# Forming P-Q in SBUF by an accumulating transfer instead of two matmuls, in 62 pair steps of a Fourier mix with a squared-ReLU feed-forward

## The chip, the cores and the metric

The kernel runs on one core of a Trainium2 chip. TensorE (PE in the profile; its weight loads are PEld) multiplies, VectorE (DVE) and ScalarE (ACT) work element by element, GpSimd (POOL) and SyncE (SP) issue the transfers. The metric is the device time of one execution in microseconds (us): 633.91, the median of three runs (633.72 to 635.05).

## The reference

```python
def _attn_ref(x):                      # x: (8, 3008, 256) float32
    X = np.fft.fft(x, axis=1)
    X = np.fft.fft(X, axis=2)
    return X.real.astype(np.float32)

def _moe_ref(x, w_in, w_out):          # x: (24064, 256), w_in: (256, 2048), w_out: (2048, 256)
    h = np.maximum(x @ w_in, 0.0)
    return (h * h @ w_out).astype(np.float32)
```

The real part of a two-dimensional Fourier transform of each of 8 batches goes, row by row, through a feed-forward layer with squared ReLU.

## The kernel before

**What is multiplied.** The transform over the 256 features is folded into the first weight matrix: the tile `gh` holds, for each of the 2048 hidden units, a cosine part (index 0), a sine part (index 1) and the sine part times -2 (index 2), over 128 rows d. The transform over the sequence gives `Z`, kept as two tiles of 128 rows d: `zc` (cosine) and `zs` (sine). Row 0 of `zs` has no sine term and carries instead the cosine term of d = 128. With P = `gh[0]`ᵀ`zc` and Q = `gh[1]`ᵀ`zs`, the hidden values of sequence row k are P + Q. Those of the mirrored row S - k are P - Q, except that the term of d = 128 keeps its sign. So one column of Z serves two rows of the output. The factor in `gh[2]` is -2 for every d but 0, and 0 there (`turn2`), so that adding `gh[2]`ᵀ`zs` to P + Q gives just that.

**Windows and steps.** The 12040 columns are cut into 25 windows, w = 0 to 24; windows 6 to 23 are 512 columns wide. A window has 8 pair steps, s = 0 to 7; each forms two chunks of 128 hidden units for all columns of the window, in one PSUM tile `ph` of 128 x 1024 float32 (two such tiles take turns). In a step of the kernel before:

- `pq(s)`: four matmuls of 512 columns (L684, L685) give P + Q;
- `square(s, 0)`: ScalarE takes the ReLU out of PSUM into `h1` (L694; three buffers), VectorE squares it into the first half of `h2` (L696);
- `others(s)`: what is spread over the steps. Always the second layer of the *previous* window: `ffn2_steps` (L596), 16 matmuls of 256 columns a step, two jobs of 8, the first over hidden chunks 0 to 7 and the second over 8 to 15, so that the first group of a window reads all of the previous window's `h2` in step 0. At odd steps ScalarE moves the result to `osb` (L611), and SyncE stores it. Further the Z matmuls of the next window (L478, in `z_steps`, with copies on ScalarE and VectorE), and the folding of a batch, below;
- `turn(s)`: two matmuls of 512 columns with `gh[2]` (L690) turn `ph` into P - Q; they must wait until ScalarE has read P + Q;
- `square(s, 1)`: the same as above, read backwards, into the second half of `h2`.

Both tiles of `h2` and of `ph` alternate. The program is written in its final order: within each engine instructions run in the order in which they are recorded.

**Folding a batch.** In windows 5, 8, 10, 13, 16 and 19 (`fold_at`) VectorE also folds a whole batch (`fold_steps`): L349, L358, L353, L361, L368, L375, L379, one or so a step. In step 2, right behind L353, GpSimd issues the load of the next batch (`load_x`, L125 and L130: one direct transfer and two gathers, 1.5 MB of float16 in SBUF; for two of the batches one of these is patched at its edge, L147 or L141, after a wait for the gather). Window 19 has no next batch. In step 6 GpSimd writes `ev` to a scratch tensor (L381), and in step 7 it waits for that and reads it back by four transfers (L389, L391). In windows 6, 9, 12, 15, 18 and 21 (`late_at`) VectorE folds what came back (L404, L415).

All transfers that GpSimd issues go to one software queue (q0 in the profile); the stores of SyncE go to another.

Of the kernel before, what the change touches and what calls it, by code (L numbers as in the profile page):

```python
# [28 lines left out]
def kernel(  # L29
# [14 lines left out]
    nc = tc.nc  # L44
    B, S, D = x.shape
    _, F = moe_w_in.shape
# [7 lines left out]
    NFC = F // P  # L54
    WN = 512

    FIRST = [240, 512, 376, 376, 512, 448]
    R23 = float(2.0 ** 23)

    RQ = (1, 3, 5, 0, 2, 4)  # L60

# [11 lines left out]
    wins = []  # L73
    g = 0
    while g < TOT:
        n = min(FIRST[len(wins)] if len(wins) < len(FIRST) else WN, TOT - g)
        wins.append((g, n))
        g += n
    NW = len(wins)

    def win_of(col):
        return max(w for w in range(NW) if wins[w][0] <= col) if col < TOT else NW
# [17 lines left out]
    const = ctx.enter_context(tc.tile_pool(name="const", bufs=1))  # L100
    tmp = ctx.enter_context(tc.tile_pool(name="tmp", bufs=2))
# [8 lines left out]
    ps_h = ctx.enter_context(tc.tile_pool(name="ps_h", bufs=2, space=bass.MemoryType.PSUM))  # L110
    ps_o = ctx.enter_context(tc.tile_pool(name="ps_o", bufs=2, space=bass.MemoryType.PSUM))
# [56 lines left out]
    perm = [const.tile([P, P], F16, name=f"perm{i}") for i in range(2)]  # L168
# [3 lines left out]
    nc.gpsimd.memset(idx["c"][0:2, :], P - 3)  # L172
    idx["f"] = iota([P, 1], [[1, 1]], -1, 1, "idx_f")
    nc.gpsimd.memset(idx["f"][0:1, :], 0)
    w16 = [const.tile([P, 2, F // 2], F16, name=f"w16_{i}") for i in range(2)]
    for i in range(2):
        nc.gpsimd.dma_start(out=w16[i], in_=moe_w_in[:, i * F // 2 : (i + 1) * F // 2].rearrange("(c p) f -> p c f", p=P))
    wout16 = const.tile([P, NFC, D], F16, name="wout16")
# [2 lines left out]
    def small(shape, name):  # L181
        return const.tile(shape, F32, name=name)
# [22 lines left out]
    def table_steps(e):  # L205
# [31 lines left out]

# [44 lines left out]
    at = const.tile([P, 2, P + 1], F32, name="at")  # L282
    for c in range(2):
        nc.scalar.activation(at[:, c, :], drow, AF.Copy, bias=R23, scale=dvs[:, c : c + 1])
    nc.vector.tensor_scalar(out=at, in0=at, scalar1=-R23, scalar2=-float(D), op0=ALU.add, op1=ALU.mult)
    for c in range(2):
# [141 lines left out]
    gh = const.tile([P, 3, F], F16, name="gh")  # L428
# [17 lines left out]
    def gh_turn(cc):  # L446
        f0 = cc * 512
        nc.vector.tensor_scalar(out=gh[:, 2, f0 : f0 + 512], in0=gh[:, 1, f0 : f0 + 512], scalar1=turn2[:, 0:1], scalar2=None, op0=ALU.mult)
# [3 lines left out]
    def zwin(w):  # L452
        if w not in zc:
            zc[w] = zp.tile([P, WN], F16, name="zc", tag="zc")
            zs[w] = zp.tile([P, WN], F16, name="zs", tag="zs")
        return zc[w], zs[w]
# [101 lines left out]
    for cc in range(1, F // 512):  # L558
        gh_turn(cc)

    def store(osb, p0, g0, m, minus, eng=nc.sync):

        for b, k0, kstep, n, c0 in runs:
            il, ih = max(g0, c0) - c0, min(g0 + m, c0 + n) - 1 - c0
            if minus and k0 in (0, H):
                il = max(il, 1)
            cnt = ih - il + 1
            if cnt <= 0:
                continue
            if minus:  # L570
                lo = p0 + (m - 1) - (c0 + ih - g0)
                row = b * S + S - (k0 + kstep * ih)
            else:
# [56 lines left out]
    def fold_jobs(i):  # L630
        f = folds[i] = fold_steps(i)
        return [f["d_even"], f["n_cos"], f["d_odd"], f["n_sin"], f["odds"], f["nyq"], f["even"], f["back"]]

    fold_at, late_at = {}, {}
    for i in range(2, B):
        fold_at[win_of(col_of[i, 0]) - 2] = i
        late_at[win_of(col_of[i, 1]) - 2] = i
    NST = NFC // 2
    old = None
    for w in range(NW):  # L640
        g0, wn = wins[w]
        h2 = h2p.tile([P, NFC, 2 * WN], F16, name="h2", tag="h2")
        zcw, zsw = zwin(w)

        lo, hi = 0, NST - 1
        at = [[] for _ in range(NST)]
        post = [[] for _ in range(NST)]
        if w == 0:
            at[2] = [f0s["even"], f0s["back"]]
        elif w == 1:  # L650
            fj = fold_jobs(1)
            at = [[f] for f in fj[0:5]] + [[], [], []]
            post[5] = fj[5:6]
            lo, hi = 6, 7
        elif w == 2:
            te = table_steps(1)
            at = [[folds[1]["even"], lambda: te["freq"](), lambda: te["args"](0)], [lambda: te["turns"](0)], [lambda: te["mods"](0)],
                  [lambda: te["absm"](0)], [lambda: te["sins"](0)], [lambda: te["coss"](0)], [], [lambda: te["weigh"]()]]
            for st in range(4):
                at[st + 3] = at[st + 3] + f0s["late"][st : st + 1]  # L660
            at[7].append(folds[1]["back"])
        elif w in fold_at:
            fj = fold_jobs(fold_at[w])
            at = [[f] for f in fj[0:5]] + [[], fj[6:7], fj[7:8]]
            post[5] = fj[5:6]
        elif w == win_of(col_of[1, 1]) - 1:
            for st in range(4):
                at[st] = folds[1]["late"][st : st + 1]
            lo = 4
        if w in late_at:  # L670
            for st in range(4):
                at[st + 2] = at[st + 2] + folds[late_at[w]]["late"][st : st + 1]
        zj, zl = [], []
        for u in need[w + 1]:
            zu = z_steps(u)
            zj += [(zu, 0, 0), (zu, 1, 0), (zu, 0, 1), (zu, 1, 1)]
        f2 = ffn2_steps(*old) if old else []
        phs = {}

        def pq(s):  # L680
            ph = phs[s] = ps_h.tile([P, 2, 512], F32, name="ph", tag="psh")
            for a in range(2):
                f0 = (2 * s + a) * P
                nc.tensor.matmul(ph[:, a, 0:wn], gh[:, 0, f0 : f0 + P], zcw[:, 0:wn], start=True, stop=False)  # L684
                nc.tensor.matmul(ph[:, a, 0:wn], gh[:, 1, f0 : f0 + P], zsw[:, 0:wn], start=False, stop=True)  # L685

        def turn(s):
            for a in range(2):
                f0 = (2 * s + a) * P
                nc.tensor.matmul(phs[s][:, a, 0:wn], gh[:, 2, f0 : f0 + P], zsw[:, 0:wn], start=False, stop=True, skip_group_check=True)  # L690

        def square(s, sg):
            h1 = h1p.tile([P, 2, 512], F16, name="h1", tag="h1")
            nc.scalar.activation(h1[:, :, 0:wn], phs[s][:, :, 0:wn], AF.Relu)  # L694
            hv = rev_dim(h1[:, :, 0:wn], 2) if sg else h1[:, :, 0:wn]
            nc.vector.tensor_tensor(h2[:, 2 * s : 2 * s + 2, sg * wn : (sg + 1) * wn], hv, hv, op=ALU.mult)  # L696

        def others(s):
            for j in at[s]:
                j()  # L700
            for j in spread(f2, s, NST):
                j()
            for j in post[s]:
                j()
            if s == lo:
                zl[:] = [j for zu, part, h in zj for j in zu(part, h)]
            if s >= lo:
                for j in spread(zl, s - lo, hi - lo) if s < hi else []:
                    j()


        ng = 2 if w == 0 or wins[w - 1][1] < 384 < wn else 1
        for s0 in range(0, NST, ng):
            ss = range(s0, s0 + ng)
            for s in ss:
                pq(s)
            for s in ss:
                square(s, 0)
            others(s0)
            for s in ss:  # L720
                turn(s)
            for s in ss:
                square(s, 1)
            for s in ss[1:]:
                others(s)
        old = (w, h2)
    for j in ffn2_steps(*old, tail=True):
        j()
# [30 lines left out]
```

## Time and profile before

| | |
|---|---|
| median of three runs | 633.91 us |
| span of the profiled execution | 632.0 us |
| TensorE busy | 615.9 us, 97% |
| ScalarE busy | 457.4 us, 72% |
| VectorE busy | 369.5 us, 58% |
| GpSimd busy | 76.5 us, 12% |
| window 0 starts at | 21.7 us |
| window 6 starts at | 140.1 us |
| window 24 starts at | 595.5 us |

A window starts with its first L684 matmul. The profile gives for each group of instructions its line, engine, output and inputs, count, busy time and mean duration, and the idle time of the engine just ahead of it with what ended that idle time. A matmul of 512 columns shows a duration of 379 ns, but the next one starts some 215 ns after it: they overlap, so the distance of starts is what one costs in a dense stream. The same holds to a smaller degree on ScalarE and VectorE, where independent neighbours overlap by about 0.1 us.

### The profile page before, as it was taken

The page shows a single profiled execution, that of the slowest core. Times are in us where ns is not written, and L with a number is a line of the kernel's source. Part 1 is how long each engine was busy: PE and PEld are TensorE (multiplying, and loading weights), DVE is VectorE, ACT ScalarE, POOL GpSimd, SP SyncE. Part 2 cuts the span into 40 slices and gives each one's busy share as a digit, 9 for nine tenths or more (in the row PEclk, how much of TensorE's full clock was granted, in tenths as well). Part 3 has the DMA queues.
Part 4 walks back from the last instruction along what each step waited for, and adds up shares of the span by engine and source line. Part 5 has one row for each costly group of instructions (what it writes and reads, how often), then busy time and mean ns, then how long its engine had stood idle before and what let it go on. Part 6 is the DMA issues. An engine that isn't in the chain of part 4 may idle for free.

```text
span 632.0 us, 11586 instructions
## 1 busy us (share of the span) xinstructions
PE 615.9 (97%) x4548; PEld 439.1 (69%) x4548; DVE 369.5 (58%) x604; ACT 457.4 (72%) x610; POOL 76.5 (12%) x125
## 2 busy tenths in 40 slices
PE   5899999999999999999999999999999999999997
PEld 2457776776777767767777677777677776777786
DVE  7887656765457557645576455854557555454430
ACT  7787778777777677767777777777777777777662
POOL 5352200022002200220011100030000200000000
PEclk9999999999999999999999999999999999999999
DMA  8936211172112711631127211262111311111112
GB/s 146 211 82 127 85 34 34 50 164 78 36 43 58 184 46 42 144 97 35 51 44 160 74 52 39 59 151 73 40 31 55 111 34 47 38 46 35 49 54 65
DMA packets 36525, 47.52 MB, mean 75 GB/s; under 512 B 4216, under 2 KB 30328, under 8 KB 36472
## 3 DMA queue, kind: packets, MB, share of 16 engines
q0 software_dynamic: 9344, 22.14, 17.6%
q1 hardware_dynamic: 26899, 24.44, 12.7%
q8 instruction: 35, 0.57, 0.4%
q10 hardware_dynamic: 228, 0.21, 0.1%
q14 instruction: 19, 0.15, 0.1%
HBM read 33.63 MB, written 27.84 MB: 97 GB/s over the span
## 4 chain that ended last, share of the span: by engine, by line
PE 93%; DVE 3%; ACT 2%; issue 1%; POOL 0%; ACTq 0%; POOLq 0%; DVEq 0%
PE po L596 51%; PE ph L684 12%; PE ph L685 12%; PE ph L690 12%; PE pz L478 4%; ACT h L694 1%; PE pw L301 1%; DVE h L696 1%; PE pg L436 0%; ACT cos L259 0%; DVE fe L349 0%; DVE fo L353 0%; ACT sin L248 0%; ACT gh L440 0%; DVE od L368 0%
## 5 line engine op out<-in xcount | busy, mean ns | idle before, releaser
L694 ACT ACTIVATE h<-ph 128x1024 f16<-128x1024 f32 (+4 forms) x400 | 368.4, 974 | 80.0 <-PE ph L690 72.1
L696 DVE TENSOR_TENSOR h<-h 128x1024 f16<-128x1024 f16 (+4 forms) x400 | 262.4, 660 | 231.6 <-ACT h L694 228.2
L596 PE MATMUL po<-wout,h 128*128 128x256 f16 (+1 forms) x3024 | 361.6, 273 | 0.0
L596 PEld LDWEIGHTS <-h 128*128 128x128 f16 (+1 forms) x3024 | 296.8, 98 | 71.3
L684 PE MATMUL ph<-zc,gh 128*128 128x512 f16 (+4 forms) x400 | 145.9, 366 | 1.1 <-ACT h L694 0.8
L685 PE MATMUL ph<-zs,gh 128*128 128x512 f16 (+4 forms) x400 | 145.9, 366 | 0.4 <-ACT zs L487 0.4
L690 PE MATMUL ph<-zs,gh 128*128 128x512 f16 (+4 forms) x400 | 112.8, 366 | 2.0 <-ACT h L694 1.5
L611 ACT ACTIVATE osb<-po 128x512 f32<-128x512 f32 (+3 forms) x95 | 54.9, 582 | 57.4 <-PE po L596 52.4
L685 PEld LDWEIGHTS <-gh 128*128 128x128 f16 x400 | 39.1, 98 | 43.8 <-issue 2.5
L684 PEld LDWEIGHTS <-gh 128*128 128x128 f16 x400 | 39.0, 98 | 41.8 <-issue 0.5
L690 PEld LDWEIGHTS <-gh 128*128 128x128 f16 x400 | 37.2, 97 | 12.7 <-issue 4.3
L421 POOL COPY xt<-xt 128x2 f16<-128x2 f16 x16 | 2.5, 186 | 173.2 <-DVE xt L404 173.2
L130 POOL DMA_INDIRECT xo<-in_x_dram,idx_r x15 | 22.1, 1471 | 4.6 <-issue 4.6
L125 POOL DMA_DIRECT2D xo<-in_x_dram x8 | 6.0, 751 | 109.8 <-DVE fo L353 109.8
L483 ACT ACTIVATE es<-pz 128x376 f32<-128x376 f32 (+1 forms) x32 | 15.4, 481 | 5.3 <-PE pz L478 5.2
L391 POOL DMA_INDIRECT rb<-scr,idx_r x16 | 18.5, 1158 | 4.9 <-issue 4.9
L487 ACT ACTIVATE zs<-pz 128x376 f16<-128x376 f32 (+23 forms) x27 | 8.5, 358 | 9.9 <-PE pz L478 9.9
L349 DVE TENSOR_TENSOR fe<-xo 128x3072 f16<-128x3072 f16 x8 | 14.3, 1786 | 1.6 <-DMA xo<-in_x_dram,idx_r 1.3
L353 DVE TENSOR_TENSOR fo<-xo 128x3072 f16<-128x3072 f16 x8 | 14.2, 1779 | 0.0
L494 DVE SCALAR_TENSOR_TENSOR zc<-es,pz 128x376 f16<-128x376 f32 (+20 forms) x26 | 9.4, 392 | 7.2 <-ACT zc L487 7.0
L301 PE MATMUL pw<-spn 128*128 128x384 f16 x30 | 8.2, 448 | 5.2 <-DVE spn L290 5.2
L389 POOL DMA_DIRECT2D rb<-scr x16 | 8.8, 551 | 33.4 <-DMA scr<-ev 33.0
(106 smaller groups left out, 220.4 us busy)
## 6 DMA issues: line engine op xcount, KB each, us to landing
out_dram<-osb SPq DMA_DIRECT2D x77, 128.0 KB
xo<-in_x_dram POOLq DMA_DIRECT2D x7, 768.0 KB, 7.0
scr<-ev POOLq DMA_DIRECT2D x8, 390.0 KB, 4.4
rb<-scr POOLq DMA_DIRECT2D x16, 130.0 KB, 5.1
out_dram<-osb SPq DMA_DIRECT2D x12, 94.0 KB
w<-in_moe_w_in_dram POOLq DMA_DIRECT2D x2, 512.0 KB, 10.0
wout<-in_moe_w_out_dram POOLq DMA_DIRECT2D x1, 1024.0 KB, 14.5
out_dram<-osb SPq DMA_DIRECT2D x8, 75.0 KB
```

What stands on the lines that cost most here:

```text
L130: nc.gpsimd.indirect_dma_start(out=flat(q), out_offset=None, in_=bass.AP(tensor=x.tensor, offset=0, ap=[[XW, B * S * D // XW], [1, XW]]), ...
L301: nc.tensor.matmul(pw[:, 0 : 3 * P], spn[:, 0, 0, :], spn.rearrange("p c r d -> p (c r d)")[:, 0 : 3 * P], start=True, stop=True)
L391: nc.gpsimd.indirect_dma_start(out=rb[:, q].rearrange("p r d -> p (r d)"), out_offset=None, in_=bass.AP(tensor=src.tensor, offset=src.offs ...
L478: nc.tensor.matmul(ps[:, o0:o1], lhs, tab, start=(h == 0 and k == 0), stop=last, skip_group_check=True)
L483: nc.scalar.activation(es[:, 0:n], ps[:, 0:n], AF.Copy, bias=0.0, scale=1.0)
L596: nc.tensor.matmul(po[0:m, j * D : (j + 1) * D], h2[:, fc, q : q + m], wout16[:, fc, :], start=(fc == 0), stop=(fc == NFC - 1))
L611: nc.scalar.activation(osb[0:mm].rearrange("p s d -> p (s d)")[:, lo:hi], po[0:mm, lo:hi], AF.Copy, bias=0.0, scale=HS * HS)
L684: nc.tensor.matmul(ph[:, a, 0:wn], gh[:, 0, f0 : f0 + P], zcw[:, 0:wn], start=True, stop=False)
L685: nc.tensor.matmul(ph[:, a, 0:wn], gh[:, 1, f0 : f0 + P], zsw[:, 0:wn], start=False, stop=True)
L690: nc.tensor.matmul(phs[s][:, a, 0:wn], gh[:, 2, f0 : f0 + P], zsw[:, 0:wn], start=False, stop=True, skip_group_check=True)
L694: nc.scalar.activation(h1[:, :, 0:wn], phs[s][:, :, 0:wn], AF.Relu)
L696: nc.vector.tensor_tensor(h2[:, 2 * s : 2 * s + 2, sg * wn : (sg + 1) * wn], hv, hv, op=ALU.mult)
```

## The change

In 62 pair steps (windows 6 to 23: steps 0, 2, 3 and 5 of a window without a batch fold, steps 1 and 3 of windows 8, 10, 13, 16 and 19) the two `turn` matmuls are gone. Such a step now runs thus:

- `half_q`: two matmuls give Q alone in `ph`. ScalarE copies -2Q to `sn[:, 0]`. VectorE forms the missing d = 128 term in `sn[:, 1]` by two `tensor_scalar` (row 0 of `zs`, spread over 128 partitions in `eb`, times `wv`, twice row 0 of `gh[1]` per hidden unit). GpSimd issues a transfer that adds `sn[:, 1]` onto `sn[:, 0]` (128 x 1024 float16, SBUF to SBUF). `sn` has two buffers, which take the place of the loaded first weight matrix.
- `others` as before, then `half_p`: two matmuls add P; ScalarE copies P + Q to the first half of `hd`.
- two steps later, `half_d`: VectorE adds `hd` and `sn[:, 0]` into the second half of `hd` backwards, takes the maximum with 0 over both halves (128 x 2048), and squares both into `h2`.

In steps that keep the old form, the first square of steps 1 and 4 (or of 0, 4 and 6 in the five windows with a fold) moves from VectorE to ScalarE. Window 3 gets 16 one-column matmuls for `wv`. In step 7 of each window from 5 to 22 SyncE issues the transfer that fills `eb`.

```diff
+    MANY, FEW = (0, 2, 3, 5), (1, 3)
+    SQ_MANY, SQ_FEW = (1, 4), (0, 4, 6)
...
+    def row_weights():
+
+        pv = ps_o.tile([P, 512], F32, name="pv", tag="po")
+        for fc in range(NFC):
+            nc.tensor.matmul(pv[:, fc : fc + 1], gh[:, 1, fc * P : (fc + 1) * P], perm[0][:, P - 1 : P], start=True, stop=True)
+        nc.vector.tensor_scalar(out=wv, in0=pv[:, 0:NFC], scalar1=2.0, scalar2=None, op0=ALU.mult)
...
+    def row_spread(w):
+
+        wn = wins[w][1]
+        t = eb[w] = tmp.tile([P, WN], F16, name="eb", tag="kf")
+        src = zwin(w)[1][0:1, 0:wn]
+        nc.sync.dma_start(out=t[:, 0:wn], in_=bass.AP(tensor=src.tensor, offset=src.offset, ap=[list(src.ap[0]), [0, P], [1, wn]]))
...
+    def halved(w):
+
+        if wins[w][1] < WN or w < 6:
+            return ()
+        return FEW if w in fold_at else MANY
...
-            nc.vector.tensor_tensor(h2[:, 2 * s : 2 * s + 2, sg * wn : (sg + 1) * wn], hv, hv, op=ALU.mult)
+            if sg == 0 and s in by_act:
+                nc.scalar.activation(h2[:, 2 * s : 2 * s + 2, 0:wn], hv, AF.Square)
+            else:
+                nc.vector.tensor_tensor(h2[:, 2 * s : 2 * s + 2, sg * wn : (sg + 1) * wn], hv, hv, op=ALU.mult)
+
+        two = halved(w)
+        by_act = () if not two else SQ_FEW if w in fold_at else SQ_MANY
+        sns, hds = {}, {}
+
+        def half_q(s):
+            ph = phs[s] = ps_h.tile([P, 2, 512], F32, name="ph", tag="psh")
+            for a in range(2):
+                f0 = (2 * s + a) * P
+                nc.tensor.matmul(ph[:, a, 0:wn], gh[:, 1, f0 : f0 + P], zsw[:, 0:wn], start=True, stop=True)
+            i = ROT[0] % 2
+            sn = sns[s] = const.tile([P, 2, 2, WN], F16, name=f"sn{i}", tag=f"w16_{i}")
+            nc.scalar.activation(sn[:, 0, :, 0:wn], ph[:, :, 0:wn], AF.Copy, bias=0.0, scale=-2.0)
+            for a in range(2):
+                nc.vector.tensor_scalar(out=sn[:, 1, a, 0:wn], in0=eb[w][:, 0:wn], scalar1=wv[:, 2 * s + a : 2 * s + a + 1], scalar2=None, op0=ALU.mult)
+            nc.gpsimd.dma_start(out=sn[:, 0, :, 0:wn].rearrange("p a n -> p (a n)"), in_=sn[:, 1, :, 0:wn].rearrange("p a n -> p (a n)"), accum_op=ALU.add)
+
+        def half_p(s):
+            ph, sn = phs[s], sns[s]
+            for a in range(2):
+                f0 = (2 * s + a) * P
+                nc.tensor.matmul(ph[:, a, 0:wn], gh[:, 0, f0 : f0 + P], zcw[:, 0:wn], start=False, stop=True, skip_group_check=True)
+            hd = tmp.tile([P, 2, 2 * WN], F16, name="hd", tag=("tt", "tm")[ROT[0] % 2])
+            ROT[0] += 1
+            nc.scalar.activation(hd[:, :, 0:wn], ph[:, :, 0:wn], AF.Copy, bias=0.0, scale=1.0)
+            hds[s] = hd
+
+        def half_d(s):
+            sn, hd = sns[s], hds.pop(s)
+            nc.vector.tensor_tensor(rev_dim(hd[:, :, wn : 2 * wn], 2), hd[:, :, 0:wn], sn[:, 0, :, 0:wn], op=ALU.add)
+            nc.vector.tensor_scalar(out=hd, in0=hd, scalar1=0.0, scalar2=None, op0=ALU.max)
+            nc.vector.tensor_tensor(h2[:, 2 * s : 2 * s + 2, :], hd, hd, op=ALU.mult)
...
+            if s0 == hi and w + 1 < NW and halved(w + 1):
+                row_spread(w + 1)
+            if s0 in two:
+                half_q(s0)
+                if s0 - 2 in hds:
+                    half_d(s0 - 2)
+                others(s0)
+                half_p(s0)
+                continue
             for s in ss:
                 pq(s)
             for s in ss:
                 square(s, 0)
+            if s0 - 2 in hds:
+                half_d(s0 - 2)
             others(s0)
...
+        for s in sorted(hds):
+            half_d(s)
```

More of the change, by code (lines that the diff above doesn't have):

```diff
@@ L174 @@
     nc.gpsimd.memset(idx["f"][0:1, :], 0)
-    w16 = [const.tile([P, 2, F // 2], F16, name=f"w16_{i}") for i in range(2)]
+    w16 = [const.tile([P, 2, F // 2], F16, name=f"w16_{i}", tag=f"w16_{i}") for i in range(2)]
     for i in range(2):
@@ L559 @@
         gh_turn(cc)
+    wv = small([P, NFC], "wv")
+    def row_weights():
[3 more added lines that the diff above has]
+        nc.vector.tensor_scalar(out=wv, in0=pv[:, 0:NFC], scalar1=2.0, scalar2=None, op0=ALU.mult)
+    eb = {}
+    def row_spread(w):
[3 more added lines that the diff above has]
+        nc.sync.dma_start(out=t[:, 0:wn], in_=bass.AP(tensor=src.tensor, offset=src.offset, ap=[list(src.ap[0]), [0, P], [1, wn]]))
     def store(osb, p0, g0, m, minus, eng=nc.sync):
@@ L638 @@
     NST = NFC // 2
+    def halved(w):
+        if wins[w][1] < WN or w < 6:
+            return ()
+        return FEW if w in fold_at else MANY
+    ROT = [0]
     old = None
@@ L672 @@
                 at[st + 2] = at[st + 2] + folds[late_at[w]]["late"][st : st + 1]
+        if w == 3:
+            at[0].append(row_weights)
         zj, zl = [], []
```

## The prediction

> **What bounds the kernel now.** I read the engine totals and the chain of waits first.
>
> ```profile
> span 632.0 us, 11586 instructions
> PE 615.9 (97%) x4548; PEld 439.1 (69%) x4548; DVE 369.5 (58%) x604; ACT 457.4 (72%) x610; POOL 76.5 (12%) x125
> PE 93%; DVE 3%; ACT 2%; issue 1%; POOL 0%; ACTq 0%; POOLq 0%; DVEq 0%
> ```
>
> TensorE sets the end. Next the windows one by one (busy us of PE, PEld, DVE, ACT, POOL, each with its count; clock; DMA share; GB/s): windows 8 (fold and load), 12 (no Z matmuls) and 16 (fold, load, Z).
>
> ```profile
> 190.51:214.90 24.39, 24.39 (x180) 17.27 (x179) 18.19 (x25) 17.48 (x21) 3.98 (x4) 1.00 0.55 124
> 292.94:317.27 24.33, 24.33 (x177) 17.21 (x176) 12.98 (x20) 17.46 (x21) 0.63 (x4) 1.00 0.14 44
> 393.41:418.96 25.55, 25.55 (x199) 18.41 (x198) 19.05 (x27) 19.20 (x27) 5.16 (x6) 1.00 0.43 85
> ```
>
> TensorE has no gap in any of them, and its clock is full. So a matmul less is worth its whole pitch, and any new wait of TensorE is paid in full. The timeline of two neighbouring steps gives the pitch:
>
> ```profile
> 269.90 0.38 PE L684 MATMUL ph<-zc,gh 128*128 128x512 f16 x1
> 270.10 1.94 ACT L694 ACTIVATE h<-ph 128x1024 f16<-128x1024 f32 x2 [1.20 <-PE ph L690]
> 270.11 0.38 PE L685 MATMUL ph<-zs,gh 128*128 128x512 f16 x1
> 270.76 1.91 PE L596 MATMUL po<-wout,h 128*128 128x256 f16 x16
> ```
>
> A 512-column matmul costs 0.215 us (starts at 269.90, 270.11), the 16 of L596 1.75. An old step is 6 x 0.215 + 1.75 = 3.04 us, a new one 4 x 0.215 + 1.75 = 2.61. ScalarE's two reads (of `turn` of the step before, and of this step) end 2.14 us after the step's start (270.10 + 1.94 = 272.04).
>
> **Gain.** 62 x 2 x 0.215 = 26.7 us of TensorE. The 16 matmuls for `wv` cost about one weight load each (L596's PEld, 98 ns): +1.6.
>
> **What hides the new work.** VectorE, per new step: two multiplies of 512 (the L448 row below; two of them took 0.64), an add like L696 (0.69), a maximum of 2048, a square of 2048. The square: L696 takes 0.692 for 1024 and L349 1.786 for 3072, so 0.69 + 0.53 = 1.22. No row has the maximum; between 0.63 (slope from L265's 0.315 for 377 to L448's 0.34 for 512) and four L448 (1.36), I take 0.70, since both rows are of its kind. That is 3.25 for the two squares of 0.69 it replaces: +1.9 a step. Window 12: 13.0 + 4 x 1.9 - 2 x 0.7 = 19.2 of 22.6 us; window 16: 19.05 + 3.8 - 2.1 = 20.8 of 24.7. It fits. ScalarE keeps its count of large reads and gains 2 or 3 squares of about 1.0 (like L694, 1.03 for this shape): window 12 19.5 of 22.6, window 16 22.2 of 24.7. It fits too, so neither becomes the bound by its sum. What decides is when things are ready.
>
> **Small waits of ScalarE (+6).** Before, `turn` came 0.865 + 1.75 = 2.61 after the step's start, ScalarE was ready at 2.14. Now `half_p` comes at 0.43 + 1.75 = 2.18: slack 0.04. Behind an odd step (its `osb` copy, 0.60) ScalarE starts some 0.1 later, and in step 2 it carries a square of step 1 besides (about 0.4). Some 0.45 a window, in 13 windows: 6.
>
> **End of the 13 windows with four new steps (+10).** `half_d(5)` stands behind `square(7, 0)` on VectorE. Step 7 starts at 4 x 2.61 + 3 x 3.04 = 19.57; ScalarE is through at 21.7, VectorE's square at 22.4, then 0.69 + 0.70 + 1.22 with its own waits: 25.05. The next window starts at 22.6, and its second job of L596 reads chunk 10 (step 5's) at 22.6 + 0.43 + 0.87 + 0.22 = 24.1. TensorE waits 0.95 in 7 such windows; 0.55 in 5 before an old first step; 0.8 before window 24: 10.2.
>
> **The transfer.** No row shows an accumulating transfer. From issue to landing a plain one on this queue (`scr`, 390 KB; ours writes 256 and reads it twice):
>
> ```profile
> L448 DVE TENSOR_SCALAR gh<-gh,turn x4: 337/341/376, 20.9 to 24.1; 128x512 f16<-128x512 f16 x4
> DMA to landing us min/median/max: 2.4/4.3/7.5
> ```
>
> I take the median, 4.3, as it is the size nearest, and keep 2.4 and 7.5. Issued at 2.2 it lands 6.5 after its step's start; `half_d(0)` can't start before 8.0 (VectorE squares step 1 first), so the wait costs nothing there, with 1.4 to spare. But the queue is shared:
>
> ```profile
> 201.51 0.75 POOL L125 DMA_DIRECT2D xo<-in_x_dram  x1 [42.59 <-DVE fo L353]
> 204.53 0.96 POOL L130 DMA_INDIRECT xo<-in_x_dram,idx_r  x1 [0.30 <-issue]
> 212.86 0.60 POOL L381 DMA_DIRECT2D scr<-ev  x1 [7.37 <-DVE ev L379]
> 216.06 1.09 POOL L389 DMA_DIRECT2D rb<-scr  x2 [2.60 <-DMA scr<-ev]
> 218.99 0.98 POOL L391 DMA_INDIRECT rb<-scr,idx_r  x1 [0.30 <-issue]
> ...
> 404.92 1.16 POOL L130 DMA_INDIRECT xo<-in_x_dram,idx_f  x1 [16.96 <-DVE fo L353]
> 413.51 0.97 POOL L130 DMA_INDIRECT xo<-in_x_dram,idx_r  x1 [0.30 <-issue]
> 416.79 0.59 POOL L381 DMA_DIRECT2D scr<-ev  x1 [2.31 <-DVE ev L379]
> 424.58 1.10 POOL L389 DMA_DIRECT2D rb<-scr  x2 [7.20 <-DMA scr<-ev]
> ```
>
> The write of `scr` alone keeps GpSimd waiting 2.60 us; issued 3.3 us behind a gather, 7.20. So a transfer waits for those issued before it. And the load fills all engines:
>
> ```profile
> 203.00:212.00 9.00, 9.00 (x69) 6.42 (x67) 5.91 (x10) 6.24 (x8) 2.19 (x2) 1.00 1.05 201
> ```
>
> **Windows 8, 10, 13, 16: step 3's transfer stands behind the load (+28.5).** In program order the load of step 2 comes first on GpSimd. In window 8 it is issued 11 us into the window and its data fill the engines until 21.5; the transfer lands at about 23. `half_d(3)` is due at 17.4 in step 5, behind `square(5, 0)`, and VectorE's queue stands for 5.5 us. Behind it: `nyq`, `square(5, 1)`, `ev`, the squares of 6 and 7. ScalarE's read of step 7 needs the `h1` buffer of `square(5, 1)`, done at 26.3 (23 + half_d 2.6 + 0.7), reads until 27.4; `turn(7)` was due at 23.1: TensorE loses 4.4. Window 10: 3.6, being longer by Z. In 13 and 16 GpSimd also waits for a gather (the step from 404.92 to 413.51), the last data come 28.5 into the window, the transfer lands at 30: 10.4 and 10.1.
>
> **Windows 6, 9, 11, 14, 17, 20: step 0's transfer stands behind the `rb` reads (+12).** GpSimd issues those for 3.9 us (216.06 to 219.97) after the wait for `scr`, which in load windows itself comes later, since `ev` does. Window 9: starts at 27.9 on window 8's scale; `ev` 27.3, `scr` landed 30.5, `rb` issued until 34.4 and landed by 37; the transfer lands 11.5 into window 9, its add ends at 12.2. ScalarE's copy of step 3 needs that `sn` buffer at 9.4, so `half_p(3)`, due 10.9, runs at 13.4: 2.5. The same sum gives 2.0 for window 6, 2.5 for 11, 2.2 for 14 and 17, 0.3 for 20: 11.7.
>
> `eb` (128 KB, SyncE, step 7) is needed only when VectorE is through with `half_d(5)`, and costs nothing; the stores queued behind it have three buffers.
>
> [...] The longest of GpSimd's gathers took 4.84 us, beside VectorE's `tensor_tensor` (L361, L368); the one beside the first L448, a one-source operation (starts 20.50 and 20.87), took 0.98, as the quickest do. [...]
>
> **Sum.** -26.7 + 1.6 + 6 + 10.2 + 28.5 + 11.7 = +31.3: span 663.3. The median of the runs lies 1.9 above the span: **665 us**.
>
> **Rivals.**
> 1. *The transfers on the shared queue don't hold each other up (faster).* Then the 28.5 + 11.7 go: 623.1 + 1.9 = 625. It decides by whether step 3's transfer lands before 17.4 in the load windows. For it: from 212.0 to 213.5 the DMA share is 0.52, so some of the 16 engines are through with the load earlier. Against: `scr`'s 7.20.
> 2. *Nothing waits at all.* Only the matmuls count: 632.0 - 26.7 + 1.6 + 1.9 = 609. Against: the 0.04 and -0.95 of slack.
> 3. *The accumulating transfer is slow*, 7.5 us to landing. `half_d(0)` then starts at 9.7 and holds ScalarE's copy for step 3 (+1.0), and `half_d(5)` comes 1.4 later: 2.4 in 13 windows, +31: 696. For it: it reads twice and computes. Against: 256 KB is less than `scr`.
> 4. *It cancels out*: half of the queue terms are absorbed and the small waits don't come: within 0.2% of 634.
>
> **How the numbers follow.** Forecast 0.47, rival 1 0.18, rival 2 0.09, rival 3 0.23, rival 4 0.03. Two runs of this kernel can differ by 0.2%. Faster 0.27, same 0.03, slower 0.70. The range goes from 620, a little under rival 1 (two thirds of rival 2's and some of rival 1's chance lie below), to 698, rival 3; the forecast's own is 640 to 680.
>
> **What would show it.** L690 falls from 400 to 276 matmuls. If the forecast holds, TensorE idles some 55 us in windows 6 to 24; window 8 ends 3 to 4 us later than 24.4, windows 13 and 16 are 34 to 36 us long; VectorE's longest waits are for `sn` by a DMA, in step 5 of the load windows (5 to 13 us) and step 2 behind `rb`; windows 12, 15, 18 are 23 to 24. If 13 and 16 are no longer than 26, the queue term is wrong; if window 12 or 18 is over 26, the transfer itself is slower than 4.3.

## The result, and the profile after

The changed kernel takes 732.48 us (median of 4 runs, 732.15 to 734.37), the kernel before 634.06 beside it: a ratio of 1.156 [1.154, 1.157]. It is slower, as forecast, but by 98 us and not by 31; the time lies outside the range. Engine totals, and the granted clock of TensorE in 40 slices, of the kernel after:

```profile
span 730.5 us, 11618 instructions
PE 622.6 (85%) x4440; PEld 436.3 (60%) x4440; DVE 441.6 (60%) x750; ACT 499.9 (68%) x651; POOL 136.5 (19%) x187
PEclk9999999989989999889997999879998999999999
```

The span grew by 98.5 us. TensorE did 108 matmuls fewer and yet was busy for 6.7 us more, and its idle time went from 16.1 to 107.9. So 91.8 us are new waits, and the rest is something else: the clock row has 7s and 8s where the kernel before had full speed throughout (mean 0.944 against 1.000). The prediction's matmuls saved and added come to 25.1 us less work, which would leave 25.1 + 6.7 = 31.8 us for the lower clock. The clock record gives a little less: 55.7 us of TensorE's busy time lie in stretches at half clock, half of which, 27.8 us, is lost. Run 3 below agrees with that: with the same 4440 matmuls and a clock of 0.997 it was busy for 593.9 us, 28.7 fewer. So some 28 us went to the lower clock.

The windows 8, 12, 14, 16 and 21 of the kernel after (busy us of PE, PEld, DVE, ACT, POOL, each with its count; clock; DMA share; GB/s):

```profile
199.74:237.31 37.57, 26.37 (x176) 17.69 (x175) 21.80 (x31) 21.02 (x24) 6.11 (x6) 0.89 0.54 90
328.60:352.61 24.01, 22.96 (x169) 16.35 (x168) 17.90 (x30) 19.43 (x23) 4.93 (x8) 1.00 0.55 93
383.46:424.22 40.76, 26.56 (x182) 18.17 (x181) 20.82 (x37) 21.27 (x29) 7.39 (x9) 0.87 0.50 95
448.22:481.10 32.88, 27.44 (x196) 19.04 (x194) 17.05 (x24) 22.15 (x30) 6.16 (x7) 0.90 0.45 73
609.13:633.14 24.01, 22.96 (x170) 16.34 (x169) 17.78 (x30) 19.43 (x23) 5.40 (x8) 1.00 0.51 87
```

Windows 12, 15 and 21 take 24.01 and differ from the forecast by hundredths: 22.6 of work, 1.0 of wait at their start and 0.36 in step 2. Window 8 was forecast 3 to 4 us longer and is 13 us longer; window 14 takes 40.8 against 26.2. No engine is near its bound in the long ones: TensorE is busy 26.6 of 40.8. What TensorE and VectorE waited for (total us, times, longest):

```profile
DVE h L730 <- ACT h L725: 128.6, 105, 6.3
...
DVE hd L760 <- DMA sn<-sn: 109.6, 23, 16.6
...
PE po L617 <- DVE h L762: 33.2, 13, 5.8
...
PE ph L752 <- ACT sn L743: 24.9, 16, 6.4
...
PE po L617 <- DVE od L378: 21.4, 2, 12.6
DVE sn L745 <- DMA eb<-zs: 20.6, 10, 6.8
...
PE ph L721 <- ACT h L725: 12.0, 7, 5.4
```

All four waits of TensorE end in VectorE's queue or in a buffer that VectorE frees. VectorE's longest total is still its wait for ScalarE's `h1`, 128.6 us, but that was 228.2 in the kernel before. What is new is its wait for the accumulating transfer into `sn` (L746), 109.6 us, and for `eb`, 20.6. The line of that transfer, from its issue to its landing:

```profile
DMA to landing us min/median/max: 3.2/4.4/10.2
```

The median is what the forecast took (4.3); the spread is what it left out. The instructions on VectorE were sized rightly (mean ns last but one):

```profile
L762 DVE TENSOR_TENSOR h<-hd 128x2048 f16<-128x2048 f16 x62 | 76.0, 1225 | 2.1
...
L761 DVE TENSOR_SCALAR hd<-hd 128x2048 f16<-128x2048 f16 x62 | 43.1, 695 | 2.1
```

How a wait on TensorE is paid twice is seen in the timeline of window 6 (start, duration, count; in brackets the idle time before and what ended it):

```profile
158.68 1.01 PE L752 MATMUL ph<-zc,gh 128*128 128x512 f16 x2 [6.38 <-ACT sn L743]
159.48 0.63 PE L715 MATMUL ph<-zc,gh 128*128 128x512 f16 x1
159.91 0.63 PE L716 MATMUL ph<-zs,gh 128*128 128x512 f16 x1
160.34 0.63 PE L715 MATMUL ph<-zc,gh 128*128 128x512 f16 x1
```

After 6.38 us of waiting, matmuls of 512 columns start 0.43 us apart, twice the 0.215 of before. Two windows of 4 us in window 8, the first behind a wait of 5.80 us that ended at 207.65:

```profile
208.00:212.00 4.00, 4.00 (x17) 2.23 (x15) 3.17 (x7) 1.94 (x2) 0.00 (x0) 0.51 0.00 1
212.00:216.00 4.00, 4.00 (x33) 3.01 (x31) 1.51 (x4) 2.43 (x3) 0.85 (x1) 1.00 0.39 67
```

Busy throughout in both, TensorE does 17 matmuls at clock 0.51 and then 33 at 1.00. The clock record has 14 such stretches, each 3.41, 6.83 or 10.24 us long and each begun in or right behind a wait, the shortest of 2.46 us and the longest of 12.60; no such stretch came with the waits of up to 1.60 us within the windows. The wait need not be as long as the stretch: the waits of 2.46 and 2.92 us came with stretches of 3.41 and 6.83. At some 28 us the lower clock is 3.8% of the span, since the waits come again and again.

### The profile page after: what moved, and what is told of

It is laid out like the page before. It is cut to its first block, busy times and chain, and to the rows that moved or that the text cites. A ratio compares the mean times of both kernels' runs of the same rounds, so it can differ in the third digit from the quotient of the medians.

```text
span 730.5 us, 11618 instructions
## 1 busy us (share of the span) xinstructions
PE 622.6 (85%) x4440; PEld 436.3 (60%) x4440; DVE 441.6 (60%) x750; ACT 499.9 (68%) x651; POOL 136.5 (19%) x187
## 5 line engine op out<-in xcount | busy, mean ns | idle before, releaser
L617 PE MATMUL po<-wout,h 128*128 128x256 f16 (+1 forms) x3024 | 378.2, 279 | 54.6 <-DVE h L762 33.2
L725 ACT ACTIVATE h<-ph 128x1024 f16<-128x1024 f32 (+4 forms) x276 | 253.9, 952 | 102.4 <-PE ph L721 56.1
L730 DVE TENSOR_TENSOR h<-h 128x1024 f16<-128x1024 f16 (+4 forms) x235 | 146.8, 635 | 132.3 <-ACT h L725 128.6
L746 POOL DMA_DIRECT2D sn<-sn x62 | 55.9, 922 | 303.6 <-DVE sn L745 116.0
L760 DVE TENSOR_TENSOR hd<-hd,sn 128x1024 f16<-128x1024 f16 x62 | 42.7, 688 | 109.8 <-DMA sn<-sn 109.6
L715 PE MATMUL ph<-zc,gh 128*128 128x512 f16 (+4 forms) x276 | 101.8, 371 | 1.1 <-ACT h L725 0.8
L716 PE MATMUL ph<-zs,gh 128*128 128x512 f16 (+4 forms) x276 | 101.5, 370 | 0.4 <-ACT zs L490 0.4
L755 ACT ACTIVATE hd<-ph 128x1024 f16<-128x1024 f32 x62 | 63.6, 1026 | 42.0 <-PE ph L752 41.8
L721 PE MATMUL ph<-zs,gh 128*128 128x512 f16 (+4 forms) x276 | 79.0, 372 | 12.3 <-ACT h L725 12.0
L743 ACT ACTIVATE sn<-ph 128x1024 f16<-128x1024 f32 x62 | 63.4, 1023 | 24.1 <-DVE hd L760 24.1
L762 DVE TENSOR_TENSOR h<-hd 128x2048 f16<-128x2048 f16 x62 | 76.0, 1225 | 2.1
L632 ACT ACTIVATE osb<-po 128x512 f32<-128x512 f32 (+3 forms) x95 | 54.6, 579 | 32.0 <-PE po L617 29.5
L745 DVE TENSOR_SCALAR sn<-eb,wv 128x512 f16<-128x512 f16 x124 | 38.0, 349 | 20.6 <-DMA eb<-zs 20.6
L761 DVE TENSOR_SCALAR hd<-hd 128x2048 f16<-128x2048 f16 x62 | 43.1, 695 | 2.1
L728 ACT ACTIVATE h<-h 128x1024 f16<-128x1024 f16 x41 | 43.3, 1057 | 1.3
L752 PEld LDWEIGHTS <-gh 128*128 128x128 f16 x124 | 12.3, 101 | 31.2 <-issue 28.7
## 6 DMA issues: line engine op xcount, KB each, us to landing
w<-in_moe_w_in_dram POOLq DMA_DIRECT2D x2, 512.0 KB, 10.6
```

The lines of the kernel that those rows point to most:

```text
L617: nc.tensor.matmul(po[0:m, j * D : (j + 1) * D], h2[:, fc, q : q + m], wout16[:, fc, :], start=(fc == 0), stop=(fc == NFC - 1))
L632: nc.scalar.activation(osb[0:mm].rearrange("p s d -> p (s d)")[:, lo:hi], po[0:mm, lo:hi], AF.Copy, bias=0.0, scale=HS * HS)
L743: nc.scalar.activation(sn[:, 0, :, 0:wn], ph[:, :, 0:wn], AF.Copy, bias=0.0, scale=-2.0)
L746: nc.gpsimd.dma_start(out=sn[:, 0, :, 0:wn].rearrange("p a n -> p (a n)"), in_=sn[:, 1, :, 0:wn].rearrange("p a n -> p (a n)"), accum_op=A ...
L755: nc.scalar.activation(hd[:, :, 0:wn], ph[:, :, 0:wn], AF.Copy, bias=0.0, scale=1.0)
L762: nc.vector.tensor_tensor(h2[:, 2 * s : 2 * s + 2, :], hd, hd, op=ALU.mult)
```

## The experiments

The theories: the load and the `rb` reads on GpSimd's queue, made larger by what follows them (B, the recorded one); the transfer `eb` holding the DMA engines (A); and, formed after the first four runs, stores that sit on a single DMA engine (D).

**1. `eb` without a transfer.** In `row_spread`, VectorE clears the tile:

```diff
-        src = zwin(w)[1][0:1, 0:wn]
-        nc.sync.dma_start(out=t[:, 0:wn], in_=bass.AP(...))
+        nc.vector.memset(t[:, 0:wn], 0.0)
```

> The transfers that fill eb are gone; eb is set to zero by VectorE instead, so that the d = 128 term is left out in the 62 new steps. All else is as in the changed kernel, the accumulating transfers included. Theory A (the eb transfer reads one partition 128 times, holds the DMA engines for some 5 us and so delays step 5's accumulating transfer): the waits in step 0 of windows 8, 13, 16, 18, 19, 22 and 23, some 30 us above the 1 us of the other windows with the halved clock behind them, go: about 702 us. Theory B (all waits come from the load and the rb reads ahead in the queue): no change, 730 to 734. Theory C (the accumulating transfer is slow by itself): no change, 730 to 734.

Measured: 687.4 us (684.7 to 692.2), ratio 1.083 [1.076, 1.089]. That is 45 us off the changed kernel, from a transfer that the forecast priced at nothing. What it does shows in the changed kernel from 346 to 357 us, cut in 40 slices of 0.275 us (tenths of the 16 DMA engines' time, then GB/s, then what was issued: KB each, us to landing):

```profile
DMA  2100000353499999989291946939193551233224
GB/s 52 22 15 0 0 0 15 97 104 78 89 179 246 246 227 231 212 153 63 7 48 4 48 15 22 34 11 45 7 41 15 26 22 26 67 97 112 82 52 127
...
sn<-sn POOLq DMA_DIRECT2D x1, 256.0 KB, 9.6
...
eb<-zs SPq DMA_DIRECT2D x1, 128.0 KB
```

In slices 13 to 17 full engines move 212 to 246 GB/s. From the 19th to the 30th those with a 9 move 34 to 63: the engines are taken, and little passes. That is `eb`, 128 reads of the same 1 KB row in one partition, issued at 348.0: by the packet records the 1 KB packets on SyncE's queue take 0.50 us each (median) from 351.0 to 354.5, against 0.06 just before. The transfer for step 5, issued at 347.0 on the other queue, ends in 16 packets of 4 bytes, one for each share of it. Fifteen of them are through by 351.1 and the last at 356.3, behind `eb` and then behind stores issued from 353.0 on; the transfer counts as landed after 9.6 us. VectorE waits 3.92 us for it, and TensorE then 4.70 us at the start of window 13. The same from the wider view of windows, with the engines' share and GB/s last:

```profile
351.00:354.00 3.00, 3.00 (x24) 2.13 (x22) 1.39 (x2) 2.67 (x5) 0.06 (x1) 1.00 0.83 27
```

0.83 of the engines' time for 27 GB/s. But windows 18, 19 and 23 still waited in this run, with no `eb` transfer to blame: theory A is a part, not the whole.

**2. No accumulating transfer,** with `eb` and its multiplies kept:

```diff
-            nc.gpsimd.dma_start(out=sn[...], in_=sn[...], accum_op=ALU.add)
```

> The 62 accumulating transfers are gone (the d = 128 term is left out), the eb transfers and VectorE's multiplies stay. Theories A and B: VectorE's half_d waits for nothing but ScalarE, the load windows and the windows behind rb lose their waits; what is left is the multiplies' wait for eb, up to 6.8 us on VectorE in ten windows, of which a part reaches TensorE: 625 to 645 us. Theory C: 624 us. If it stays above 660, the waits are not those of the transfers.

Measured: 632.97 us, ratio 0.997 [0.996, 0.999]. Without that one line 99.5 us are gone: the loss comes of VectorE waiting for it, and `eb`, the load and the stores harm through it alone, apart from some 9 us (against run 3). In those VectorE's multiplies wait for `eb` itself, for up to 9.8 us, mostly in windows 11 and 17.

**3. Neither of the two.**

> Neither eb transfers nor accumulating transfers (the d = 128 term is left out); matmuls, ScalarE's and VectorE's work of the new steps all stay. All theories of transfers: 632.0 - 26.7 + 1.6 + 4.7 (step 2, 0.36 us in 13 windows) + 10.2 (end of 13 windows) = 621.8 of span, 624 us of time, TensorE's clock full throughout. If VectorE or ScalarE were the bound instead: above 634.

Measured: 623.96 us (623.12 to 624.80), ratio 0.982 [0.980, 0.985]. The sum of the prediction without its two queue terms is 625 (its rival 1). So the sum of the matmuls saved, the wait in step 2 and the end of the window stands as written.

**4. No new step behind the load.** The windows with a load keep one new step, ahead of it:

```diff
-    MANY, FEW = (0, 2, 3, 5), (1, 3)
+    MANY, FEW = (0, 2, 3, 5), (1,)
```

> The five windows with a fold have one new step (1) instead of two (1 and 3), so no accumulating transfer stands behind the load of the next batch. Theory B: the waits of TensorE in windows 8, 10, 13, 14, 16 and 17 that end with step 3's transfer go, some 32 us, and about 12 us of halved clock behind them, less 2 us for ten more matmuls: about 690 us. Theory A or C alone: 2 us more than the changed kernel, 734.

Measured: 710.1 us (706.9 to 716.3), ratio 1.122 [1.116, 1.127], 20 us short of what B needs. The four waits of the load windows are gone (in the changed kernel 5.41, 5.05, 12.60 and 8.82, together 31.9), but TensorE now waits longer in step 3 of others: that of window 11 takes 9.6 us there and 11.8 here, of window 14 4.5 and 8.6, of window 17 4.3 and 10.0. In window 14 step 0's transfer stands behind the `rb` reads, as B has it. In 11 and 17 VectorE first stands 9.0 and 9.1 us for `eb`, which SyncE issues within 2.5 us of those reads, and only then does step 0's transfer go out. In all VectorE waits for `eb` in this run (total, times, longest)

```profile
DVE sn L745 <- DMA eb<-zs: 36.7, 13, 9.1
```

where it was 20.6 in the changed kernel. Whether the `rb` reads hold `eb` up was not tried. The waits of the other causes stay.

**5. Stores split.** The rows of a store go out in two pieces, the first a multiple of 16 rows:

```diff
-            eng.dma_start(... cnt rows from lo ...)
+            whole = cnt // 16 * 16
+            for c0_, n_ in ((0, whole), (whole, cnt - whole)):
+                if n_:
+                    eng.dma_start(... n_ rows from lo + c0_ ...)
```

> The changed kernel with one edit: a store whose row count is no multiple of 16 goes out as two, the multiple of 16 and the rest. Theory D (a store of an odd row count runs on one DMA engine for several us, and the accumulating transfer's share on that engine lands 7 to 8 us after its issue, though the other shares were there after 4): waits in windows 7, 17, 18, 19, 22 and 23 shrink, some 15 to 25 us with the halved clock behind them: 705 to 718 us. If stores don't matter: 732.

Measured: 677.9 us (676.7 to 679.6), ratio 1.069 [1.066, 1.072]. 54.6 us less than the changed kernel for an edit of the stores, which no compute engine waits for there: more than run 1 or run 4 takes off, and more than expected. The stretch that had led to it, of run 1 from 505 to 518 us in 40 slices of 0.325 us:

```profile
DMA  3479985510008588987322000023000000000000
GB/s 44 66 126 164 135 164 113 117 44 25 22 22 79 63 135 151 132 170 132 82 60 50 25 22 22 19 72 88 19 16 25 22 25 22 25 25 22 25 25 25
...
sn<-sn POOLq DMA_DIRECT2D x1, 256.0 KB, 7.1
out_dram<-osb SPq DMA_DIRECT2D x1, 113.0 KB
```

From the 23rd slice on the share is 0, that is under a tenth, in all but two, while 16 to 25 GB/s pass without a break; and in the last microsecond alone the share reads (window of run 1, share and GB/s last)

```profile
516.00:517.00 1.00, 0.00 (x0) 0.00 (x0) 0.96 (x3) 0.97 (x2) 0.00 (x0) 1.00 0.07 25
```

0.07 of 16 engines is one engine. Stores of 113, 79 and 49 rows of 1 KB are issued in this stretch. By the packet records the accumulating transfer, issued at 507.9, is through by 512.0 but for its last eight packets of 2 KB, which begin between 513.0 and 515.0: a last share behind the stores. This one harms nobody, as VectorE comes to it only at 516.05. The transfer before it, issued at 503.27, does: fifteen of its sixteen shares are through by 508.0, the last at 510.7, and VectorE waits for it (the idle time in brackets):

```profile
511.09 0.69 DVE L759 TENSOR_TENSOR hd<-hd,sn 128x1024 f16<-128x1024 f16 x1 [3.70 <-DMA sn<-sn]
```

So these stores show one engine's share (0.07) and one pace (22 to 25 GB/s), and in run 5, with a first piece of a multiple of 16 rows, 54.6 us are gone. By what rule a row count puts a store on one engine, and which one, was not shown.

In the run with split stores the landing times of the line are

```profile
DMA to landing us min/median/max: 3.2/3.8/9.8
```

and VectorE's wait (total, times, longest)

```profile
DVE hd L763 <- DMA sn<-sn: 58.0, 13, 15.0
```

The median fell from 4.4 to 3.8 and 109.6 us of waiting to 58.0. The waits at the start of windows 8, 13, 16, 18, 19, 22 and 23 are gone but for the 1.0 us forecast; what stays is the load (8, 10, 14, 17) and `rb` (6, 20).

**6. All three at once:** `eb` cleared, one new step in the load windows, stores split.

> Three edits together: no eb transfers (eb is zero, the d = 128 term is left out), one new step in the five fold windows (nothing stands behind the load), stores split at a multiple of 16. What is left of the transfers' waits is the rb reads ahead of step 0's transfer. Theory B with the recorded size: 624 + 2 for the ten matmuls + 12 = 638 us. If A, B and D name all causes, it lies between 626 and 645; above 660 another cause is missing.

Measured: 635.6 us (632.0 to 639.1), ratio 1.001 [0.999, 1.003]. Landing times:

```profile
DMA to landing us min/median/max: 3.2/3.7/5.2
```

Of the 57 transfers the profile gives the landing of 43, and none of these takes longer than 5.2 us from its issue. Of the new waits over 2 us there remain those in step 3 of windows 14 and 17, behind `rb`, each with a slow step after it. Taken one at a time the three edits bring 45 + 22 + 55 = 122 us, together 97, so that some of it is counted twice; a likely reason, not shown window by window, is that two causes held up the same transfer.

**7. The addition on GpSimd, not by a transfer.** `eb` comes from a matmul with a matrix whose only row of ones is row 0:

```diff
-            nc.gpsimd.dma_start(... accum_op=ALU.add)
+            nc.gpsimd.tensor_tensor(sn[:, 0, :, 0:wn], sn[:, 0, :, 0:wn], sn[:, 1, :, 0:wn], op=ALU.add)
```

> A complete kernel without the accumulating transfers: GpSimd adds sn[:, 1] onto sn[:, 0] by a tensor_tensor of 128x1024, eb comes from one matmul a window with a selecting weight tile and a VectorE copy; new steps 0, 2, 3, 5 and 1 in fold windows; ScalarE squares in steps 4 and 6. If the waits of the transfers were all that was wrong: 632.0 - 24.6 + 1.6 + 4 (18 matmuls for eb) + 10 (end of 13 windows) = 623 of span, 625 us. If GpSimd's add takes over 4 us or holds VectorE: above 640.

Measured: 694.2 us (692.0 to 695.8), ratio 1.094 [1.091, 1.098]: a miss. Groups of this kernel (busy us, mean ns, idle before):

```profile
L750 POOL TENSOR_TENSOR sn<-sn 128x1024 f16<-128x1024 f16 x57 | 139.9, 2455 | 229.0 <-DVE sn L749 219.9 <-ACT osb L636 3.4 <-ACT hd L759 3.1
...
L765 DVE TENSOR_SCALAR hd<-hd 128x2048 f16<-128x2048 f16 x57 | 109.9, 1928 | 2.0
```

The maximum on VectorE, 695 ns beside the transfer, takes 1928 on the mean in this run, where GpSimd's add takes 2455. Of the 57 maxima, 18 touch no add and take 0.69 us; the other 39 lie under an add for 1.94 to 1.95 us and take 2.49 to 2.50. The edit changed nothing in the maximum itself, only its company. VectorE is late by it, and TensorE waits 22.2 us for its `h2` at the windows' starts and 25.4 us for it in the matmul that makes `eb`.

**8. The addition on VectorE.** One operation multiplies and adds in place, so that two multiplies and the transfer go; the halves are summed one step later, not two; three and one new steps in a window; `eb` by the same matmul at the start of step 7:

```diff
-                nc.vector.tensor_scalar(out=sn[:, 1, a, 0:wn], in0=eb[w], scalar1=wv[...], op0=ALU.mult)
-            nc.gpsimd.dma_start(... accum_op=ALU.add)
+                nc.vector.scalar_tensor_tensor(out=sn[:, 0, a, 0:wn], in0=eb[w], scalar=wv[...], in1=sn[:, 0, a, 0:wn], op0=ALU.mult, op1=ALU.add)
-                if s0 - 2 in hds:
-                    half_d(s0 - 2)
+                if s0 - 1 in hds:
+                    half_d(s0 - 1)
```

> A complete kernel without the accumulating transfers: VectorE adds the d = 128 term by two scalar_tensor_tensor (512 each, about 0.6 us) instead of two multiplies; eb from a matmul; new steps 0, 2 and 4 (1 in fold windows), summed one step later, so that nothing is late at the window's end; ScalarE squares in steps 5 and 6. Gain 44 x 0.43 = 18.9; 632.0 - 18.9 + 1.6 + 4 + 3 = 621.7 of span, 623.6 us. If the end of the windows still waits: 630.

Measured: 630.2 us (629.6 to 631.0), ratio 0.993 [0.991, 0.995]. That is 0.7% faster than before; 6.6 us of the expected gain are missing. Each of the two operations takes 0.75 us on the mean, where about 0.6 was expected. Step 6 is up to 1.3 us too long: the matmul for `eb` waits for its operand at the head of TensorE's queue, 5.5 us in its 18 windows.

**9 to 12.** The accumulating transfer kept and its causes mended without leaving anything out (stores split, `eb` by a matmul late in step 7, one new step in load windows); the split stores alone, put into the kernel before; run 8 with `eb` at the end of step 7 and two new steps in load windows; and that with four and two new steps:

```diff
 run 11
-    MANY, FEW = (0, 2, 4), (1,)
+    MANY, FEW = (0, 2, 4), (1, 5)
 run 12
-    MANY, FEW = (0, 2, 4), (1, 5)
+    MANY, FEW = (0, 2, 3, 5), (1, 5)
-    SQ_MANY, SQ_FEW = (5, 6), (0, 4, 6)
+    SQ_MANY, SQ_FEW = (4, 6), (0, 4, 6)
```

> A complete kernel that keeps the accumulating transfers with the three causes mended: stores split at a multiple of 16, eb from one matmul in step 7 and a VectorE copy instead of a transfer, one new step in the five fold windows. Theories A, B and D together: the 635.6 us of the run with the d = 128 term left out, and 4 us for 18 matmuls: 636 to 642. If a further cause hangs on the eb term: above 650.

> The kernel before with its stores split at a multiple of 16. Theory D says that a store on one DMA engine hurts only what waits for that engine, and nothing here does: 634 us, within 0.3%. If the stores cost time by themselves: faster by over 0.5%.

> As the kernel without transfers in which VectorE adds the d = 128 term (630.2 us), with the eb matmul moved to the end of step 7, where its operand has long been there, and a second new step (5) in the five fold windows. Step 6 was up to 1.3 us longer than its matmuls in that run, 11 us in all, of which 3.8 are the matmuls themselves: 629.0 - 7.2 - 2.2 = 619.6 of span, 621 us. If the wait only moves: 628.

> As the one before with four new steps (0, 2, 3, 5) in the 13 windows without a fold, ScalarE squares in 4 and 6. TensorE alone would give 5.6 us less, 615 us. VectorE's sum in window 12 is 13.0 + 4 x 2.7 - 1.4 = 22.4 of 22.8 us: if it becomes the bound, 622 us or more.

Measured: run 9, 634.9 us, ratio 1.000 [0.998, 1.002]; run 10, 633.7, ratio 0.999 [0.998, 1.001]; run 11, 622.1, ratio 0.981 [0.979, 0.983]; run 12, 617.7 (617.2 to 618.2), ratio 0.973 [0.971, 0.975].

Run 10 shows that the stores cost the kernel before nothing (633.7 us with them split, 634.0 without): their single engine became a price, 54.6 us by run 5, only when VectorE came to wait for transfers in sixteen shares. Run 9 shows that even mended, the accumulating transfer brings no gain. Run 12 beats both kernels. Its page:

```profile
span 615.8 us, 11485 instructions
PE 595.8 (97%) x4458; PEld 429.3 (70%) x4458; DVE 501.0 (81%) x768; ACT 499.6 (81%) x651; POOL 79.2 (13%) x127
...
L749 DVE SCALAR_TENSOR_TENSOR sn<-eb,wv,sn 128x512 f16<-128x512 f16 x124 | 87.5, 747 | 12.0 <-ACT sn L747 11.9
```

TensorE is at 97% again with 20 us less work. VectorE pays 0.75 us for each half of the addition, 87.5 in all where the multiplies alone took 38.0, and has the room: it is busy for 81% of the span, up to 23.65 of 25.37 us in the windows with a fold.

**13. The load by itself:** run 9 with the second new step back in the load windows, `FEW = (1, 3)`.

> The mended kernel with the transfers (634.9 us), but with steps 1 and 3 new in the fold windows as in the change: what it costs more is what step 3's transfer behind the load costs by itself. Recorded size: 28.5 us of waits less 2.2 us of matmuls, 661 us. With the halved clock behind the four waits, up to 3.4 us each, 665 to 675. If the load held nothing up without the other two causes: 633.

Measured: 662.0 us (660.3 to 663.6), ratio 1.043 [1.040, 1.046]: 27.0 us above run 9, as by the recorded size. Its windows 8 and 9 (as above, the clock third from last):

```profile
190.46:220.25 29.79, 24.53 (x176) 16.93 (x175) 21.84 (x32) 20.94 (x24) 6.12 (x6) 0.96 0.53 106
220.25:247.33 27.08, 27.08 (x182) 18.72 (x181) 17.90 (x34) 21.05 (x26) 8.63 (x12) 0.92 0.47 113
```

TensorE idles 5.26 us in window 8, and in window 9 it has no gap but a clock of 0.92; in run 9 the same windows take 24.55 and 24.84. Of the 7.5 us that this load costs, 2.2 lie in the window after it, as clock. What TensorE waited for in this run:

```profile
PE po L624 <- DVE od L378: 14.4, 2, 7.2
...
PE ph L728 <- ACT h L732: 10.8, 6, 5.1
```

Two waits of 7.2 at the start of windows 14 and 17, and the ones in step 7 of windows 8 and 10.

## Why the prediction was right in its direction and wrong in its size

The runs that differ by one cause form a ladder:

| kernel | us | step up | what the step adds |
|---|---|---|---|
| 3, no transfers | 624.0 | | |
| 9, transfers mended | 634.9 | 11.0 | transfers behind `rb`; a matmul for `eb`; five new steps fewer; stores split |
| 13, load | 662.0 | 27.0 | step 3's transfer behind the load |
| 5, split stores | 677.9 | 15.9 | `eb` by a transfer, not a matmul |
| the changed kernel | 732.5 | 54.6 | stores on one DMA engine |

Run 13 holds all that the prediction put a price on, and takes 662.0 where it said 665. The other 70.5 us are `eb` and the stores. How they divide depends on the order: in the ladder `eb` adds 15.9 and the stores 54.6; by run 1, which has no transfer for `eb` but unsplit stores, the stores add 25.4 (687.4 against 662.0, but for run 13's matmul for `eb`) and `eb` 45.1.

Right, step by step:
- *Gain, the matmuls for `wv`, the small waits of ScalarE, the end of the 13 windows.* Run 3 has them all: 624.0 against 625.0. Windows 12, 15 and 21 have the gain and the two waits one by one. The matmuls for `wv` were put at 1.6 and cost 0.17: window 3, which holds them, grew from 19.73 to 19.90.
- *What hides the new work.* The maximum 0.695 for 0.70, the square 1.225 for 1.22; neither VectorE nor ScalarE became the bound.
- *Windows 8, 10, 13, 16, behind the load.* Forecast 28.5, measured 27.0 in run 13, or about 29 when the five new steps that it has over run 9 (5 x 0.43 us) are added. The chain is the one described: in window 8 TensorE stops in step 7 for ScalarE's `h1`. For windows 13 and 16 the wait ends in `od` (L378) at the start of the next window, also queued on VectorE behind `half_d(3)`. The sum came out right by luck, as two errors cancel: the long two waits were put at 10.4 and 10.1 and are 7.2 in run 13, and nothing was put down for the clock behind each. The place was off too: in run 13 windows 14 and 17 are 35.3 and 35.9 us long, and 13 and 16 take 25.3. In the changed kernel 13 and 16 are 30.9 and 32.9, over the 26 of the sign, but for waits of 4.70 and 5.44 at their start, which run 13 with the same load doesn't have.
- *Behind `rb`.* Forecast 11.7 in six windows. In run 9 windows 14 and 17 alone are longer, by 3.8 and 4.9 over window 20 of the same kind. The kind of wait is right; the windows that have it differ from run to run (6 and 20 in run 5).
- *GpSimd's issues beside VectorE.* No term was put down for them, and none was needed: in the changed kernel the 20 issues (L746) during which a whole maximum ran took 0.92 to 0.95 us, the quickest of those that met none 0.84, some 0.1 less. In run 9 the `rb` windows 9, 11 and 20 take 24.84, which is run 3's 24.62 without any transfer and 0.22 for `eb`'s matmul.

Wrong:
- *"`eb` ... costs nothing; the stores queued behind it have three buffers."* This sentence is where most of the miss lies. It asks whether somebody waits for `eb` or for the stores, and not what else is on the DMA engines with them. For the stores the answer was right; for `eb` it was not, as VectorE waited for it ten times, up to 6.8 us. The two were put at nothing and cost 70.5 us together (by the ladder 15.9 for `eb`, or up to 20 if all 18 of the 0.22 us matmuls that stand in for it are counted, and 54.6 for the stores). On the forecast's 665 that gives 735.5: with this term the sum would have come within 3 us, in part by the luck above.
- *"I take the median, 4.3."* True as a median and wrong as a price. The transfer lands with the slowest of its sixteen shares (in the two followed above fifteen were through 2.7 and 5.2 us before the last), and the slack was 1.4 us. The bound of 7.5 was kept for the range, as rival 3, yet with the place wrong: not each transfer is slow, the median stayed at 4.4, but those that meet a store, `eb` or the load land after 6 to 10: 20 of the 54 whose landing the profile gives, and with split stores 3, all in load windows. So the sign that was to tell them apart (windows 12 and 18 over 26) read 24.0 and 27.1: the transfer's own time is right, its company is not.
- *"Any new wait of TensorE is paid in full."* It is paid in full and then again: 14 stretches at half clock, some 28 of the 98.5 us. They came with waits from every cause, so this is no term of its own in the ladder but lies in its steps.

Two readings are a little off and change nothing: the row 2.4/4.3/7.5 is of the writes and the reads of `scr` together (the writes alone have 2.8/4.4/7.5), and the two rows behind the square give 0.55 for a further 1024 and not 0.53.

How much the stores would cost without the load's transfers to fall on was not tried; the ladder gives each step on top of those above it in the table.

## What to carry to other kernels

When an engine is made to wait for a transfer, price it by the slowest of its shares (here it landed after up to 10.2 us, the median being 4.4), and look for what else uses those DMA engines at that time, on any queue, also transfers that nobody waits for: here stores of 113 or 79 rows, where splitting at a multiple of 16 took 54.6 us off, and a broadcast out of one partition, which cost 15.9 by the ladder. The longer waits on TensorE cost their length and then time at half clock: in the changed kernel each of the 14 waits of 2.46 us or more within the windows came with such a stretch, of 3.41 to 10.24 us, and none of those up to 1.60. The matmuls saved were real, and they were kept by doing the addition on an engine with room to spare instead of by a transfer: 617.7 us against 634.0.

## What the runs showed of the hardware that was not expected

- In the changed kernel a broadcast of one partition's 1 KB row to 128 partitions took most of the DMA engines' time from 351 to 354 us, with a share of 0.83 at 27 GB/s; the 1 KB packets on its queue took 0.50 us each in that time, 0.05 to 0.06 before.
- An accumulating transfer of 256 KB, issued at 347.0 us in the changed kernel, landed with the last of its 16 shares: fifteen were through by 351.1 us, the last at 356.3.
- In run 1 stores of 113 or 79 rows moved at 22 to 25 GB/s on what the share (0.07) says is one engine of 16.
- In the changed kernel the clock fell by half in 14 stretches of 3.41, 6.83 or 10.24 us in or behind a wait of TensorE, and TensorE read as fully busy in stretches of it (208 to 212 us: 4.00 of 4.00 at clock 0.51).
- In run 7, under a GpSimd `tensor_tensor` of 128x1024 (2.46 us on the mean), VectorE's maximum of 128x2048 took 2.5 us in place of 0.69.
